# A gated memory and a feed-forward layer on one core: step 3's value products move ahead of the gate transposes, and some loads, conversions and reads are put at other places

## The chip, the cores and the metric

The kernel runs on one core of a Trainium2 chip. The metric is the device time of one execution in microseconds. Before the change its median over three runs is 487.62 us. The core has five engines that each take their instructions in program order: TensorE (PE; its weight loads are listed apart as PEld), VectorE (DVE), ScalarE (ACT), GpSimd (POOL) and SyncE (SP), which here only issues DMA transfers. They wait for each other through semaphores. SBUF is the on-chip memory, PSUM the banks into which TensorE writes, DRAM the memory outside.

## What is computed

For each of 4 batches and 8 heads a recurrence runs over 768 tokens with head size 40; its output goes through a feed-forward layer of width 320 to 2048 to 320.

```
for t in range(S):                          # S = 768, for each b, h
    m_new  = maximum(f[t] + m, i[t])
    f_stab = exp(f[t] + m - m_new);  i_stab = exp(i[t] - m_new);  m = m_new
    C = f_stab * C + i_stab * outer(v[t], k[t])     # 40 x 40
    n = f_stab * n + i_stab * k[t]
    y[t] = sigmoid(o[t]) * (C @ q[t]) / maximum(abs(n @ q[t]), 1)
x = y as (4 * 768, 320)                     # tokens by (head, channel)
h = x @ w_in                                # 3072 x 2048
g = maximum(h, 0) + log1p(exp(-abs(h)))     # softplus
out = g @ w_out                             # 3072 x 320
```

All of it is in fp32.

## The kernel before, in words

**The recurrence** is worked in chunks of 128 tokens. A step is one chunk of one batch with all 8 heads; there are 24, s = 0 to 23. A name such as `3_0` or `0_4` is batch and chunk of a step: step 3 is `3_0`, step 4 is `0_1`, steps 6, 7 and 8 are `0_3`, `0_4` and `0_5`, step 10 is `1_2`. Three steps make one tile of 384 tokens; there are 8 tiles. In a step the decay factors between the tokens (`fb`, loaded from DRAM by `decays`, L436) go through a scan on VectorE (L445, two halves of 4 heads) into the decay matrix `pw`; the scores `sp` (L519, TensorE) multiply it (L521); the value products give the output before normalisation; `cp` (L496) is what the chunk adds to the state, and `cn` is the new state (copied at L503 by ScalarE for a first chunk, added at L501 by VectorE otherwise). Steps up to 5 are "plain" (`plain_step`): value products `yp` (L553), normaliser `nq` (L559 to L561), product with the output gate `sig` (L562, GpSimd) and `x` (L565), then transposes into the tile's operand X (L630 to L636). Steps from 6 on are "wide" (`wide_step`): products with the old state `iq` (L572, read at L575), value products `yq` (L583, read at L588), the result written to DRAM (`yd`, L595) and read back in another layout (`yx`, `nw`, L599 to L603), then normalised (L607 to L610) and put into X (L618 to L622). Queries and keys of a wide step are loaded as a leading part (`hiq`, `hik`, L391) and a remainder (`loq`, `lok`, L405) which are made from one load per tile (L295, `prepare`).

**The feed-forward layer** works on (tile, block) pairs (t, f), with 16 blocks of 128 hidden columns for each tile: 8 matmuls `hp` (L1000), softplus twice on ScalarE (L872 `gh`, L873), a remainder `gl` on VectorE (L876), and 9 matmuls `po` (L966) in three groups of three: `woh` with `gh`, `wol` with `gh`, `woh` with `gl`. An fp32 operand is held as a leading part and a remainder there too, and products of the two remainders are left out. Block 0 to 9 of tile 0 come first, then all 16 of tile 1, then the last 6 of tile 0; the half sums of tile 0 lie in DRAM in between (`halves`, written at L1027, read back by `get_halves` at L1035, added at L1041). Tiles 2 to 7 follow. The weights are converted piece by piece while this runs: `convert(u, 0)` makes `wih` and `wil` for blocks 2u and 2u+1, `convert(u, 1)` makes `woh` and `wol`. Each goes through ScalarE (L212 `mag`, L215 `sg`), VectorE (L217, L219, both on `sg`), ScalarE (L250, L254 or L265) and GpSimd (L257, L259 or L267).

**What sets the order.** `products()` counts the feed-forward matmuls, n. Everything else is a generator that says at which n it wants to go on; `tick(n)` lets those go on whose number has come. Each engine then executes its instructions in the order in which they were written. So tables of numbers set the order of the program on each engine, and when something happens is left to the waits: `GR` for the gates, `CW` and `CO` for the conversions, `W_...`, `SOON` and `SCAN` for wide steps, `SPD`, `IQD`, `YQD` for how many matmuls a read follows its products.

**The gates of later chunks** are transposed on TensorE once (`pg`, L189 and L191) and copied to `gT` by ScalarE (L193, L194); L196 loads the factors `flast` by which a state decays over a chunk.

**A pair of PSUM banks** serves `cp`, `pg`, `yp`, `sp`, `iq`, `yq` by turns: each new tile takes the other bank of the two, but a name in `again` takes the same bank as the tile ahead of it. A tile can be written once what read its bank's last tile is done.

Of the kernel before, what the change touches and what calls it, by code (L numbers as in the profile page):

```python
# [39 lines left out]
def mlstm_moe_kernel(  # L40
# [28 lines left out]
    class Pair:  # L69


        last = 1
        again = "sp1_0_1", "yp0_1"

        def tile(self, shape, dtype, tag, name, **_):
            self.last ^= name not in self.again
# [72 lines left out]
        nc.scalar.copy(gT[:, 0, 0, :], pg)  # L149
        yield  # L150

    GR = [4, 9, 8, 30, 47, 41, 43, 26]

    def later_gates():

# [4 lines left out]
        nc.sync.dma_start(ig, gates[1, :, L:])  # L160
        yield GR[0]
        m = p2.tile([NCHAIN, w + 1], F32, tag="eg", name="m")
        nc.vector.tensor_copy(m[:, 0:1], m_end)
        nc.vector.tensor_tensor_scan(m[:, 1:], fg, ig, m[:, 0:1], ALU.add, ALU.max)
        yield GR[0]
        nc.gpsimd.tensor_tensor(fg, fg, m[:, 0:w], op=ALU.add)
        nc.gpsimd.tensor_tensor(fg, fg, m[:, 1:], op=ALU.subtract)
        nc.gpsimd.tensor_tensor(ig, ig, m[:, 1:], op=ALU.subtract)
        yield GR[1]
        nc.scalar.activation(fg, fg, AF.Exp)  # L170
        nc.scalar.activation(ig, ig, AF.Exp)
        yield GR[2]
        d1 = p1.tile([NCHAIN, w], F32, tag="loq", name="d1")
# [5 lines left out]
        fc = d1  # L179
        yield GR[7]  # L180
        nc.vector.tensor_tensor_scan(fc, fg, d1, 0.0, ALU.mult, ALU.add)
        nc.vector.tensor_copy(fl_s, fc[:, L - 1 : w : L])
        yield GR[3]
        nc.sync.dma_start(fl_d, fl_s)
# [130 lines left out]
    NH = 2 * NG  # L315
# [54 lines left out]
    def load(z):  # L370
        t, n, gs = z.t, z.n, slice(z.g * D, (z.g + 1) * D)
        if t < PLAIN:

            if z.s < NG:
                room, tags = (p1, ("loq", "lok")) if z.s == 2 else (p2, ("qst", "kst"))
                z.qst = room.tile([128, H, L], F32, tag=tags[0], name=f"qst{n}")
                z.kst = room.tile([128, H, L], F32, tag=tags[1], name=f"kst{n}")
                padded[z.s] = z.qst, z.kst
                with tc.issue_after(eye.ins):
                    (nc.gpsimd if z.s == 2 else nc.vector).memset(z.qst, 0.0)  # L380
                    nc.gpsimd.memset(z.kst, 0.0)
            else:
                z.qst, z.kst = padded[z.s % 2]
            nc.sync.dma_start(z.qst[0:D], qk[t, 0, gs])
            nc.sync.dma_start(z.kst[0:D], qk[t, 1, gs])
        else:
            (qh, ql), (kh, kl) = parts[t]
            z.qst = p2.tile([D3, H, L], F32R, tag="qst", name=f"qst{n}")
            z.kst = p2.tile([D3, H, L], F32R, tag="kst", name=f"kst{n}")
            for r, to, part in ((0, z.qst, qh), (0, z.kst, kh), (1, z.qst, qh), (2, z.kst, kh)):  # L390
                nc.sync.dma_start(to[r * D : (r + 1) * D].bitcast(F32), part[gs].bitcast(F32))  # L391
        if t > 0:
            z.old = None
            if z.c > 0 and not stays(z.b, z.c - 1):
                z.old = p2.tile([D3, H, E2], F32, tag="cn", name=f"pk{n}")
                for r in range(3 if t >= PLAIN else 1):
                    nc.sync.dma_start(z.old[r * D : (r + 1) * D], park[z.b])
        if z.s != NG:
            load_values(z)

    def load_low(z):

        gs = slice(z.g * D, (z.g + 1) * D)
        for r, to, part in ((1, z.kst, parts[z.t][1][1]), (2, z.qst, parts[z.t][0][1])):
            nc.sync.dma_start(to[r * D : (r + 1) * D].bitcast(F32), part[gs].bitcast(F32))  # L405
# [16 lines left out]
    def decays(z):  # L422

        z.fbs = []
        h0 = z.b * H
        for i in range(2):
            if z.s < NG:
                fb = ps_h.tile([128, HG, L], F32, tag="hp", name=f"fb{z.n}_{i}")
                for j in range(HG):
                    h = h0 + i * HG + j  # L430
                    nc.tensor.matmul(
                        fb[:, j, :], ident[:, h : h + 1].broadcast_to([128, 128]), fg0, start=True, stop=True
                    )
            else:
                fb = p2.tile([128, HG, L], F32, tag="fb", name=f"fb{z.n}_{i}")
                nc.sync.dma_start(fb, fz_d[z.c, h0 + i * HG : h0 + (i + 1) * HG, :].partition_broadcast(128))  # L436
            z.fbs.append(fb)
# [36 lines left out]
    def stays(b, c):  # L474

        return ORDER.index((b, c + 1)) <= ORDER.index((b, c)) + 2
# [43 lines left out]
        yield 1 if k == 2 * NG + 1 else 2 if i and z.t == 1 else SPD  # L520
        nc.vector.tensor_tensor(z.pws[i], sp, z.pws[i], op=ALU.mult)  # L521

    SPD, IQD, YQD = 5, -8, 3

    def out_gate(z):
        if z.s < NH:
# [291 lines left out]
    def rel(g):  # L818
        for r in g:
            if type(r) is int:  # L820
                yield -1000 - r

    def wide_step(z):
        if z.s != NH + 2:
            yield W_FB
            decays(z)
        yield SOON.get(z.s, W_LOAD)
        load(z)
        yield SOON.get(z.s, W_LOW - 8) + 8
        load_low(z)  # L830
        if z.s == NH + 2:
            decays(z)
        last = z.c == NC - 1
        yw = values_wide(z)

        def y():
            for r in yw:
                if r == "write":
                    return
                yield r  # L840

        c = new_state(z)
        ev = [(SCAN.get(z.s, W_SCAN), lambda: decay(z)), (W_Y, lambda: load_decays(z))]
        if not last:
            ev += [(W_CN, lambda: old_state(z)), (W_VW, lambda: last_decays(z)), (W_VW, lambda: state_values(z))]
        if z.c > 0:
            ev += [(W_CS, lambda: stack(z))]
        ev += [(W_SP0, lambda: scores(z, 0)), (W_SP1, lambda: scores(z, 1))]
        if not last:
            ev += [(W_CP, lambda: state(z)), (W_CP + 6, lambda: next(c)), (W_CD + 6, lambda: next(c))]  # L850
        if z.c > 0:
            ev += [(W_IQ0, lambda: inter_wide(z, 0)), (W_IQ1, lambda: inter_wide(z, 1))]
        ev += [(W_VI if z.s > NH else W_CP, lambda: gate_values(z)), (W_YQ, y), (W_YD, lambda: next(yw, None)), (W_RD, lambda: read_wide(z))]

        d = AWAY
        ev += [(W_FIN + d - 1, lambda: finish_wide(z)), (W_FIN + d, lambda: end_wide(z))]
        ev.sort(key=lambda e: e[0])
        for w, f in ev:
            yield w
            r = f()  # L860
            if hasattr(r, "__next__"):
                yield from rel(r)

    SOON = {NH + 1: -62, NH + 2: -66}
    SCAN = {NH + 1: -30, NH + 2: -30}
    AWAY = 18

# [11 lines left out]
    CW = [-4, -15, 8, 12, 13, 26]  # L879
    CO = [0, 5, 8, 13, 17, 22]  # L880

    def convert(u, i):
        g = (weights_out if i else weights)(u)
        for w in (CO[:4] + [16, 21] if (u, i) == (0, 1) else CO if i else CW[:5] + [22] if u == 1 else CW):
            yield w
            next(g, None)

    def fetch(i):
        yield 20
        fetch_next()  # L890
# [21 lines left out]
    def start(g, base):  # L912
        nonlocal order
        order += 1
        resume(g, base, 0, order)
# [98 lines left out]
    SPLIT = 10  # L1014
# [16 lines left out]
    def get_halves():  # L1031
        yield 0
        for j in range(NG):
            sums[j] = result_tile(0, j)
            nc.sync.dma_start(sums[j], halves[j])  # L1035
# [24 lines left out]
    with in_order():  # L1060
        for k, (u, i) in enumerate(tensors[AHEAD:]):
            if k < 2:
                at = (-8, -4)[k]
            else:
                at = (17 - 2 * 34, 26 - 34 + 10 * (u == 4))[i] + 34 * u if u < SPLIT // 2 else (168, 192)[i] + 48 * (u - SPLIT // 2)
            start(convert(u, i), at)
            start(fetch(i), at)
        start(first_states(), 0)
        LEAD, TS = 174, 16 * 17
        EARLIER = 26  # L1070
        before = -1000
        for s in range(NG, NS):
            z = steps[s] = Step(s)
            if z.wide:
                base = TS * z.t - LEAD - EARLIER - TS * (NG - 1 - z.g) // NG if z.t > WIDE else (183, 264, 344)[z.g]
                if z.g == 0:
                    start(prepare(z.t), (base - 145, before - 54, before - 90)[min(z.t - WIDE, 2)])
                before = base
            else:
                base = [0, 40, 76][s - NG]  # L1080
            start(whole(z), base)
        for t in range(WIDE, NT):
            start(wide_gates(t), TS * (t - 1) + GP + 70 * (t == WIDE))
        start(warm_block(4, 5), 0)
        start(warm_block(9, 4), 0)
        start(get_halves(), TS + 17 * SPLIT + 40)
        zs = first_tile()
        products()

# [36 lines left out]
```

## Time and profile before

| | |
|---|---|
| runs | 487.62, 484.41 and 489.94 us, median 487.62 |
| profiled execution | 489.94 us, of which the profile's span covers 488.2 |
| mean granted TensorE clock | 0.985 |
| TensorE busy | 468.6 us, 96% of the span |
| VectorE, ScalarE, GpSimd busy | 66%, 44% and 45% |
| TensorE instructions | 3444 |

The profiled execution is the slowest of the three runs; 1.7 us of it lie outside the span. A busy TensorE includes time at a lower clock. In the profile's rows "L" and a number is a line of the kernel above, names are given as output `<-` inputs without the numbers of step and buffer, and a bracket at a row's end is the idle time of the engine just before and what ended it. SPq rows are DMA issues on SyncE.

### The profile page before, as it was taken

How to read it: one execution, taken by the hardware profiler on the slowest of the kernel's cores; microseconds unless marked ns; L12 is line 12 of the kernel's file. 1: busy time of each engine (PE TensorE's matmuls, PEld its weight loads, DVE VectorE, ACT ScalarE, POOL GpSimd, SP SyncE). 2: the span in 40 equal slices, each digit the busy share in tenths (PEclk: the TensorE clock that was granted, in tenths of full speed). 3: DMA queues.
4: the chain of work that ended last, by engine and by line, in shares of the span. 5: the costliest groups of instructions: out<-in, count | busy, mean ns of one | idle time of the engine just before them, and what ended most of it. 6: DMA issues, size and time to landing. Idle time of an engine off the chain costs nothing.

```text
span 488.2 us, 9355 instructions
## 1 busy us (share of the span) xinstructions
PE 468.6 (96%) x3444; PEld 447.6 (92%) x3444; DVE 324.6 (66%) x517; ACT 216.6 (44%) x424; POOL 218.0 (45%) x303
## 2 busy tenths in 40 slices
PE   8997999898989989999999999999999999999996
PEld 7976998798888989999999999999999999999996
DVE  8878787868678748568568659568757757542211
ACT  1656446555934524264343635263424433334232
POOL 8375558368875232652383344634375234110000
PEclk9999699999999989999999999999999999999999
DMA  6948955689957695678655874668657571001001
GB/s 180 290 146 257 232 187 183 180 236 271 209 159 200 183 238 148 174 198 214 204 159 176 218 223 122 182 193 223 170 161 198 138 225 45 17 24 42 0 1 41
DMA packets 45608, 81.11 MB, mean 166 GB/s; under 512 B 6626, under 2 KB 23482, under 8 KB 45562
## 3 DMA queue, kind: packets, MB, share of 16 engines
q1 hardware_dynamic: 38218, 68.80, 50.7%
q0 software_dynamic: 4320, 8.26, 6.7%
q10 hardware_dynamic: 3024, 3.44, 2.1%
q8 instruction: 27, 0.44, 0.4%
q14 instruction: 19, 0.16, 0.1%
HBM read 52.38 MB, written 8.80 MB: 125 GB/s over the span
## 4 chain that ended last, share of the span: by engine, by line
PE 71%; DMA 8%; DVE 5%; ACT 2%; issue 2%; SPq 1%; POOL 1%; ACTq 0%; DVEq 0%
PE hp L1000 31%; PE po L966 30%; PE yq L583 3%; PE sp L519 3%; PE cp L496 2%; PE iq L572 2%; DMA nw<-yd 2%; DMA wr<-in_w_in 1%; DMA wo<-in_w_out 1%; DMA y<-fc_d 1%; DMA fb<-fz_d 1%; DMA qst<-loq 1%; DVE sgo L217 1%; SPq L391 1%; DVE pw L445 0%
## 5 line engine op out<-in xcount | busy, mean ns | idle before, releaser
L1000 PE MATMUL hp<-X,wih 128*128 128x384 f32 x768 | 182.0, 341 | 0.4 <-ACT X L634 0.4
L872 ACT ACTIVATE gh<-hp 128x384 fp32r<-128x384 f32 x128 | 62.7, 490 | 168.5 <-PE hp L1000 149.9
L1000 PEld LDWEIGHTS hp<-X,wih 128*128 128x128 f32 x768 | 133.0, 189 | 2.2 <-issue 0.9
L876 DVE TENSOR_TENSOR gl<-hp,gh 128x384 fp32r<-128x384 f32 x128 | 70.2, 549 | 56.4 <-ACT hp L873 56.0
L966 PE MATMUL po<-woh,gh 128*128 128x320 f32 x384 | 83.5, 315 | 1.6 <-ACT gh L872 1.1
L966 PE MATMUL po<-woh,gl 128*128 128x320 f32 x384 | 84.3, 314 | 0.1
L966 PE MATMUL po<-wol,gh 128*128 128x320 f32 x384 | 83.0, 315 | 0.9 <-POOL wol L267 0.9
L445 DVE TENSOR_TENSOR_SCAN pw<-fb,ident 128x512 f32<-128x512 f32 x48 | 71.5, 1529 | 0.1
L1000 PE MATMUL hp<-X,wil 128*128 128x384 f32 x256 | 69.5, 344 | 0.0
L966 PEld LDWEIGHTS po<-woh,gh 128*128 128x128 f32 x384 | 65.3, 189 | 3.2 <-ACT gh L872 1.4
L966 PEld LDWEIGHTS po<-wol,gh 128*128 128x128 f32 x384 | 62.3, 190 | 2.5 <-issue 1.2
L966 PEld LDWEIGHTS po<-woh,gl 128*128 128x128 f32 x384 | 63.4, 190 | 0.6 <-DVE gl L876 0.4
L873 ACT ACTIVATE hp<-hp 128x384 f32<-128x384 f32 x128 | 62.2, 486 | 0.0
L595 POOL DMA_DIRECT2D yd<-y x36 | 20.8, 580 | 85.8 <-DVE y L588 84.0
L1000 PEld LDWEIGHTS hp<-X,wil 128*128 128x128 f32 x256 | 46.1, 189 | 1.1 <-issue 1.0
L575 DVE TENSOR_TENSOR y<-iq,y 41x512 f32<-41x512 f32 x36 | 24.5, 682 | 30.4 <-PE iq L572 27.9
L519 PEld LDWEIGHTS sp<-qst,kst 120*128 120x128 f32 (+1 forms) x240 | 33.6, 198 | 5.9 <-issue 3.6
L519 PE MATMUL sp<-qst,kst 120*128 120x128 f32 (+1 forms) x240 | 34.1, 277 | 4.8 <-DMA qst<-loq 2.3
L521 DVE TENSOR_TENSOR pw<-sp,pw 128x512 f32<-128x512 f32 x48 | 32.0, 682 | 5.2 <-PE sp L519 4.9
L620 ACT CAST X<-eg 128x384 fp32r<-128x384 f32 x18 | 9.2, 514 | 52.1 <-DVE eg L618 52.1
L472 POOL TENSOR_TENSOR vw<-vt,gw 128x328 f32<-128x328 f32 x19 | 15.6, 822 | 36.0 <-DVE gw L466 25.0
L501 DVE TENSOR_TENSOR cn<-cn,cp 40x328 f32<-40x328 f32 x16 | 7.8, 486 | 29.9 <-POOL cn L487 29.3
(131 smaller groups left out, 596.9 us busy)
## 6 DMA issues: line engine op xcount, KB each, us to landing
fb<-fz_d SPq DMA_DIRECT2D x42, 256.0 KB
vt<-in_vko SPq DMA_DIRECT2D x23, 324.0 KB
qst<-hiq SPq DMA_DIRECT2D x36, 160.0 KB
kst<-hik SPq DMA_DIRECT2D x36, 160.0 KB
wo<-in_w_out SPq DMA_DIRECT2D x8, 640.0 KB
wr<-in_w_in SPq DMA_DIRECT2D x8, 512.0 KB
eg<-in_oT SPq DMA_DIRECT2D x6, 576.0 KB
yd<-y POOLq DMA_DIRECT2D x36, 96.0 KB, 3.3
```

What stands on the lines that cost most here:

```text
L445: nc.vector.tensor_tensor_scan(pw.rearrange(flat), fb.rearrange(flat), ident4.rearrange(flat), 0.0, ALU.mult, ALU.add)
L472: nc.gpsimd.tensor_tensor(z.vw, v1, z.gw.broadcast_to([128, H, E]), op=ALU.mult)
L519: nc.tensor.matmul(sp[:, j, :], z.kst[:, h, :], z.qst[:, h, :], start=True, stop=True)
L521: nc.vector.tensor_tensor(z.pws[i], sp, z.pws[i], op=ALU.mult)
L575: nc.vector.tensor_tensor(y, iq, y, op=ALU.mult)
L583: nc.tensor.matmul(yq[e0:e1, p, :], z.via[:, h * E : h * E + e1 - e0], z.pws[h // HG][:, h % HG, :], start=True, stop=True)
L595: nc.gpsimd.dma_start(rows[i], z.y[i * PP : i * PP + EP])
L872: nc.scalar.activation(gh, hp, AF.Softplus)
L873: nc.scalar.activation(hp, hp, AF.Softplus)
L876: nc.vector.tensor_tensor(gl, hp, gh, op=ALU.subtract)
L966: nc.tensor.matmul(po[j], a[:, j * 128 : (j + 1) * 128], w[:, f, :], start=(first and left[j] == 2), stop=(last and left[j] == 0),)
L1000: nc.tensor.matmul(hp, a, r, start=(i == 0), stop=(i == len(seq) - 1))
```

## The change

Seven numbers or tables are changed and one generator is written differently; no instruction is added or taken away.

```
-        again = "sp1_0_1", "yp0_1"
+        again = "sp0_0_1", "sp1_0_1", "yp0_1"
-    GR = [4, 9, 8, 30, 47, 41, 43, 26]
+    GR = [4, 9, 8, 30, 50, 47, 48, 27]
-    SPD, IQD, YQD = 5, -8, 3
+    SPD, IQD, YQD = 5, -8, 1
     def wide_step(z):
-        if z.s != NH + 2:
-            yield W_FB
-            decays(z)
-        yield SOON.get(z.s, W_LOAD)
-        load(z)
-        yield SOON.get(z.s, W_LOW - 8) + 8
-        load_low(z)
-        if z.s == NH + 2:
-            decays(z)
+        soon, low = SOON.get(z.s, (W_LOAD, W_LOW))
+        at = [(W_FB + 12 * (z.s == NH + 2), decays), (soon, load), (low, load_low)]
+        for w, f in sorted(at, key=lambda e: e[0]):
+            yield w
+            f(z)
-    SOON = {NH + 1: -62, NH + 2: -66}
+    SOON = {NH + 1: (-96, -54), NH + 2: (-66, -58)}
     def convert(u, i):
         g = (weights_out if i else weights)(u)
-        for w in (CO[:4] + [16, 21] if (u, i) == (0, 1) else CO if i else CW[:5] + [22] if u == 1 else CW):
+        for w in (CO[:4] + [16, 21] if (u, i) == (0, 1) else CO[:4] + [23, 27] if (u, i) == (1, 1) else CO if i
+                  else CW[:5] + [22] if u == 1 else CW[:3] + [9, 10, 26] if u == 2 else CW):
...
-                at = (17 - 2 * 34, 26 - 34 + 10 * (u == 4))[i] + 34 * u if u < SPLIT // 2 else (168, 192)[i] + 48 * (u - SPLIT // 2)
+                at = (17 - 2 * 34, 26 - 34 + 6 * (u == 4))[i] + 34 * u if u < SPLIT // 2 else (168, 198)[i] + 48 * (u - SPLIT // 2)
...
-        start(get_halves(), TS + 17 * SPLIT + 40)
+        start(get_halves(), TS + 17 * SPLIT + 95)
```

Here NH is 6, so that `NH + 1` and `NH + 2` are steps 7 and 8. In words: the gate transposes and their copies come later (`GR`), and with them `sp0_0_1` joins the names that stay on the bank of the tile ahead; the remainder load and the output conversion of piece 1 come later and piece 2's VectorE half earlier (`convert`); the output conversions of piece 4 come 4 matmuls earlier, those of pieces 5 to 7 come 6 later; a wide value product is read 1 matmul after it instead of 3; step 7's leading loads come 34 matmuls earlier; step 8's decays go behind the next tile's loads; the half sums are loaded 55 matmuls later.

Below are three places in the program's order. The first is on GpSimd, where the feed-forward layer reaches block 2 of tile 0: `wol_99<-sgo1` is the remainder of `w_out` for blocks 2 and 3, `sig3_0` the output gate of step 3, and `vw0_1` the weighted values of step 4. Before:

```order
L259 TENSOR_TENSOR wih_96<-sgi2_477,wih_96 64x128 x2
L267 TENSOR_TENSOR wol_99<-sgo1_576,woh_98 128x640
L562 TENSOR_TENSOR sig3_0_467<-sig3_0_467,nq3_0_660 128x320
L472 TENSOR_TENSOR vw0_1_671<-vt0_1_527,gw0_1_668 128x328
L484 MEMSET cn0_1_724 128x336
```

And on GpSimd at that place after the change:

```order
L259 TENSOR_TENSOR wih_96<-sgi2_477,wih_96 64x128 x2
L562 TENSOR_TENSOR sig3_0_467<-sig3_0_467,nq3_0_658 128x320
L472 TENSOR_TENSOR vw0_1_670<-vt0_1_527,gw0_1_667 128x328
L267 TENSOR_TENSOR wol_99<-sgo1_576,woh_98 128x640
L484 MEMSET cn0_1_724 128x336
```

The remainder `wol` has moved behind step 3's `sig` and step 4's `vw`. At the same place TensorE has the following before (`pg` are the gate transposes, `yp3_0` step 3's value products, `po` the output products of block 1):

```order
L189 MATMUL pg_606<-ident4_79,ig_117 128x32 x5
L191 MATMUL pg_606<-ident4_79,d1_426 128x32 x2
L966 MATMUL po0_0_0_551<-woh_98,gh0_1_504 128x320
L966 MATMUL po0_0_1_552<-woh_98,gh0_1_504 128x320
L966 MATMUL po0_0_2_553<-woh_98,gh0_1_504 128x320
L966 MATMUL po0_0_0_551<-wol_99,gh0_1_504 128x320
L966 MATMUL po0_0_1_552<-wol_99,gh0_1_504 128x320
L553 MATMUL yp3_0_633<-vi3_0_571,pw3_0_0_439 128x41 x4
L553 MATMUL yp3_0_633<-vi3_0_571,pw3_0_1_441 128x41 x4
L966 MATMUL po0_0_2_553<-wol_99,gh0_1_504 128x320
```

TensorE at that place after the change (the lines behind the diff are numbered 4 lower there, so that L962 is L966 above):

```order
L962 MATMUL po0_0_0_551<-woh_98,gh0_1_504 128x320
L962 MATMUL po0_0_1_552<-woh_98,gh0_1_504 128x320
L962 MATMUL po0_0_2_553<-woh_98,gh0_1_504 128x320
L962 MATMUL po0_0_0_551<-wol_99,gh0_1_504 128x320
L962 MATMUL po0_0_1_552<-wol_99,gh0_1_504 128x320
L553 MATMUL yp3_0_622<-vi3_0_571,pw3_0_0_439 128x41 x4
L553 MATMUL yp3_0_622<-vi3_0_571,pw3_0_1_441 128x41 x4
L962 MATMUL po0_0_2_553<-wol_99,gh0_1_504 128x320
L189 MATMUL pg_636<-ident4_79,ig_117 128x32 x5
L191 MATMUL pg_636<-ident4_79,d1_426 128x32 x2
```

The value products and the transposes have changed places, and with them their banks: the tile ahead of both is `cp3_0`, whose bank `yp3_0` had to share before and `pg` has to share now. The third place is on SyncE, ahead of step 10's scores: `halves` are tile 0's half sums, `cn1_1` the state that step 10 starts from, `lok3` and `loq3` the remainders of tile 3. Before:

```order
L420 DMA vt1_2_1925<-in_vko 128x648
L1035 DMA ob0_0_1931<-halves_102 128x320
L1035 DMA ob0_1_1933<-halves_102 128x320
L1035 DMA ob0_2_1935<-halves_102 128x320
L507 DMA cn1_1_1856<-cn1_1_1856 40x336
L508 DMA cn1_1_1856<-cn1_1_1856 40x336
L405 DMA kst1_2_1920<-lok3_1450 40x1024
L405 DMA qst1_2_1919<-loq3_1448 40x1024
L295 DMA loq4_2041<-in_qk 120x1024
L295 DMA lok4_2043<-in_qk 120x1024
L350 DMA y1_2_2097<-fc_d_89 64x4x128
```

And on SyncE at that place after the change:

```order
L420 DMA vt1_2_1925<-in_vko 128x648
L507 DMA cn1_1_1856<-cn1_1_1856 40x336
L508 DMA cn1_1_1856<-cn1_1_1856 40x336
L405 DMA kst1_2_1920<-lok3_1444 40x1024
L405 DMA qst1_2_1919<-loq3_1442 40x1024
L295 DMA loq4_2035<-in_qk 120x1024
L295 DMA lok4_2037<-in_qk 120x1024
L1031 DMA ob0_0_2068<-halves_102 128x320
L1031 DMA ob0_1_2070<-halves_102 128x320
L1031 DMA ob0_2_2072<-halves_102 128x320
L350 DMA y1_2_2097<-fc_d_89 64x4x128
```

The three loads of half sums have moved behind six others. Besides these, on VectorE the read of step 6's `yq` (L588) and one `gl` stand ahead of `w_out` piece 6's conversion (L217, L219) instead of behind it, the state sum `cn0_4` (L501) stands ahead of piece 7's, and L219 of piece 4 stands ahead of a part of X (L636). On ScalarE, step 3's place has `mag` and `sg` of `w_in` piece 3 (L212, L215) ahead of the two copies to `gT`, and these ahead of `woh` (L265), where `woh` came first and `mag`, `sg` last. On SyncE, step 7's leading loads and values (L391, L420) stand ahead of `w_in` piece 7 and step 7's decays, behind `w_out` piece 5, and step 8's decays (L436) stand behind the two loads of tile 3 (L295) instead of ahead of them.

More of the change, by code (lines that the diff above doesn't have):

```diff
@@ L883, in convert @@
         g = (weights_out if i else weights)(u)
-        for w in (CO[:4] + [16, 21] if (u, i) == (0, 1) else CO if i else CW[:5] + [22] if u == 1 else CW):
+        for w in (CO[:4] + [16, 21] if (u, i) == (0, 1) else CO[:4] + [23, 27] if (u, i) == (1, 1) else CO if i else CW[:5] + [22] if u == 1 else CW[:3] + [9, 10, 26] if u == 2 else CW):
             yield w
```

## The prediction

> **What bounds the kernel now.** I read the page first for the busy shares, then TensorE's waits, then busy time by stages, and last the timeline and the chain around the waits that the change touches.
>
> ```profile
> PE 468.6 (96%) x3444; PEld 447.6 (92%) x3444; DVE 324.6 (66%) x517; ACT 216.6 (44%) x424; POOL 218.0 (45%) x303
> PEclk9999699999999989999999999999999999999999
> ```
>
> TensorE is busy 468.6 of 488.2 us, so only two things can be won: its idle time, and the time at a lower clock, which the strip shows in two places (6 and 8 tenths). Its waits, longest first:
>
> ```profile
> PE yp L553 <- issue: 2.6, 1, 2.6
> PE sp L519 <- DMA qst<-loq: 2.3, 1, 2.3
> ...
> PE sp L519 <- DVE y L588: 1.3, 1, 1.3
> PE po L966 <- ACT gh L872: 1.1, 1, 1.1
> PE iq L572 <- DVE cn L501: 1.1, 1, 1.1
> ...
> PE po L966 <- POOL wol L267: 0.9, 1, 0.9
> ...
> PE po L966 <- ACT woh L265: 0.5, 1, 0.5
> ```
>
> Columns: total, times, longest. Now the stages (length, busy time of each engine, then the granted clock, the DMA engines' share and GB/s):
>
> ```profile
> 49.00:58.00 9.00, 9.00 (x38) 9.00 (x39) 7.31 (x12) 2.38 (x5) 4.51 (x6) 0.52 1.01 234
> 100.00:130.00 30.00, 27.05 (x217) 24.93 (x216) 24.04 (x32) 18.05 (x34) 22.97 (x26) 1.00 0.93 247
> 172.00:178.00 6.00, 5.17 (x25) 5.20 (x26) 1.94 (x3) 1.35 (x3) 3.25 (x5) 0.72 1.04 240
> 178.00:300.00 122.00, 122.00 (x931) 117.14 (x930) 85.44 (x138) 51.62 (x101) 54.27 (x86) 1.00 0.67 186
> ```
>
> The two longest waits are each followed by slow time: 9.00 us at 0.52 lose 9.00 x 0.48 = 4.3 us of full-clock work, 6.00 us at 0.72 lose 1.7. From 178 to 300 TensorE has no gap. So whatever TensorE has gained by 178 us should reach the end; what is gained earlier can be lost at a later wait whose cause does not move with it.
>
> **Part 1, the exchange at 46 to 58 us (`GR`, `again`, conversion of piece 1).**
>
> ```profile
> 45.90 0.45 PE L966 MATMUL po<-wol,gh 128*128 128x320 f32 x2
> 48.99 3.61 PE L553 MATMUL yp<-vi,pw 128*128 128x41 f32 x16 [2.63 <-issue]
> ...
> 58.19 0.61 PE L966 MATMUL po<-wol,gh 128*128 128x320 f32 x3
> ...
> 48.48 0.42 ACT L503 COPY cn<-cp 40x328 f32<-40x328 f32 x1
> ...
> 49.62 3.90 DVE L445 TENSOR_TENSOR_SCAN pw<-fb,ident 128x512 f32<-128x512 f32 x2
> ...
> 50.60 1.83 POOL L267 TENSOR_TENSOR wol<-sgo,woh 128x640 fp32r<-128x640 f32 x1 [0.59 <-ACT woh L265]
> 54.55 0.72 POOL L562 TENSOR_TENSOR sig<-sig,nq 128x320 f32<-128x320 f32 x1 [2.12 <-DVE gw L466]
> 55.23 0.74 POOL L472 TENSOR_TENSOR vw<-vt,gw 128x328 f32<-128x328 f32 x1
> ```
>
> The wait called "issue" ends at 48.99, just when the copy that frees `cp3`'s bank ends (48.48 + 0.42 = 48.90); `yp` shares that bank. On the other bank `yp` needs no wait, and TensorE reaches `pg`, which now waits for the copy. This 2.63 us goes. What is late next is on GpSimd: `wol`, needed by the `po` group that ran at 58.19, used to run at 50.60. Now it stands behind `sig` and `vw`, which wait for VectorE's scans. The scans began at 49.62 and took 3.90 beside `wol`; with `wol` gone from beside them they should take about what the pair below takes.
>
> ```profile
> 127.80 2.32 DVE L445 TENSOR_TENSOR_SCAN pw<-fb,ident 128x512 f32<-128x512 f32 x2
> ```
>
> Taking 49.3 as their start (a little earlier than before, since VectorE has nearly the same work ahead): 2.3 for the scans, 1.0 from their end (49.62 + 3.90 = 53.52) to `sig` at 54.55 as before, 0.72 + 0.74 for `sig` and `vw`, then `wol`, some 1.5 where it took 1.83 beside a scan. That is about 55.6. TensorE, without its wait of 2.63 and the 4.3 us that the slow clock took, would want it at 58.19 - 6.9 = 51.3. So **a new wait of some 4 us** takes the old one's place, and the `po` group starts at 55.6 in place of 58.19: 2.6 earlier. Since waits of 2.6 and 2.3 us were both followed by slow clock, I charge this one too, at the smaller of the two prices: 2.6 - 1.7 = **0.9 us gained**. Bounds: no slow clock, +2.6; the larger price of 4.3, 2.6 - 4.3 = -1.7.
>
> **Part 2, VectorE's L219 of piece 4 ahead of X.**
>
> ```profile
> 87.81 0.55 DVE L636 TENSOR_TENSOR X<-xp,X 128x384 fp32r<-128x384 f32 x1
> ...
> 89.90 0.71 PE L966 MATMUL po<-woh,gh 128*128 128x320 f32 x3 [0.53 <-ACT woh L265]
> ```
>
> L219 no longer has the 0.55 us of L636 ahead of it, and TensorE's wait of 0.53 for `woh` depends on it. I take **0.4**, between 0 and 0.55. Moving the other pieces' ScalarE and GpSimd halves by a few matmuls I cost at 0: those two engines are idle over half the span, and their queues' order moves under TensorE's `hp` work; without that cover, a piece costs one `wol`, at most 1.8.
>
> **Part 3, step 6's `yq` read, step 7's loads, `cn0_4` (109 to 140 us).** The waits of 1.3 (`sp` for L588), 1.1 (`iq` for `cn` L501) and 0.4 (`cp` for `vw` behind them) go, since each reader now stands ahead of a conversion that itself waited. That is 2.8 on TensorE. But a lead has to pass this:
>
> ```profile
> 134.07 1.01 DVE L607 SCALAR_TENSOR_TENSOR nm<-nw 128x128 f32<-128x128 f32 x1 [0.88 <-DMA nw<-yd]
> ...
> 139.40 0.71 PE L966 MATMUL po<-woh,gh 128*128 128x320 f32 x3 [1.11 <-ACT gh L872]
> ...
> 126.42 7.63 DMA nw<-yd
> ...
> 119.19 1.79 SPq L436 DMA_DIRECT2D fb<-fz_d  x2
> ...
> 121.09 0.38 SPq L295 DMA_DIRECT2D loq<-in_qk  x1
> 122.13 1.02 SPq L295 DMA_DIRECT2D lok<-in_qk  x1
> ```
>
> At 139.40 TensorE waits for an activation whose engine had been busy putting step 6 into X; that chain (`nw` from DRAM 7.63 us, then five operations on VectorE) runs from 126.42, in a stretch with the DMA engines 0.93 busy. Step 7's loads start earlier, which thins that stretch, but step 8's decays `fb` now queue behind two loads of 480 KB (120 x 1024 x 4 bytes): 0.96 MB at the 247 GB/s of that stretch is 3.9 us. The scans that need them began at 127.80, and `nm` stands behind the scans on VectorE. The two about cancel, so I take **0 net**: the 2.8 us are won at 115 to 127 and given back by 140. Upper bound 2.8. For the lower one: `fb` was issued at 119.19 and now comes behind `lok`, whose issue ended at 123.15, 4.0 later; the scans would begin at 131.8 and end at 134.1, and between them and `nm` VectorE has four more operations:
>
> ```profile
> 130.04 0.52 DVE L876 TENSOR_TENSOR gl<-hp,gh 128x384 fp32r<-128x384 f32 x1
> 130.60 0.69 DVE L575 TENSOR_TENSOR y<-iq,y 41x512 f32<-41x512 f32 x1
> 131.39 0.69 DVE L588 TENSOR_TENSOR y<-yq,y 112x512 f32<-112x512 f32 x1
> 132.63 0.56 DVE L876 TENSOR_TENSOR gl<-hp,gh 128x384 fp32r<-128x384 f32 x1 [0.56 <-ACT hp L873]
> ```
>
> With their 2.5 us `nm` starts at 136.6, 2.5 later than 134.07, and TensorE's wait at 139.40 becomes 2.5 longer net of all lead; with a slow stretch at the larger price, 4.3, this is -6.8.
>
> **Part 4, the half sums behind step 10's loads (160 to 178 us).**
>
> ```profile
> 159.17 0.49 DVE L501 TENSOR_TENSOR cn<-cn,cp 40x328 f32<-40x328 f32 x1 [2.35 <-POOL cn L487]
> ...
> 160.02 5.28 SPq L1035 DMA_DIRECT2D ob<-halves  x3
> ...
> 167.71 0.71 SPq L405 DMA_DIRECT2D qst<-loq  x1
> ...
> 167.71 4.98 DMA qst<-loq
> ...
> 172.83 0.63 PE L519 MATMUL sp<-qst,kst 120*128 120x128 f32 x4 [2.31 <-DMA qst<-loq]
> ...
> 179.08 0.93 DVE L1041 TENSOR_TENSOR ob<-po,ob 128x320 f32<-128x320 f32 x2 [2.06 <-PE po L966]
> ```
>
> SyncE held the loads of half sums for 5.28 us until their buffers were free, with step 10's four loads queued behind them: the last, `qst<-loq`, went out at 167.71 and landed 4.98 later, and `sp` waited 2.31 for it. Now the four can go once `cn` is there (159.17 + 0.49 = 159.66): four issues of 0.7 put `qst<-loq` at about 161.8, and with the same 4.98, even with 2 us more, it lands by 169, ahead of 170.5 where TensorE began to wait. The wait of 2.31 goes and with it its slow stretch of 1.7: **+4.0**. The half sums queue behind two more issues, still go out at about 165.5 when their buffers are free, and are needed at 179.08: free. Bounds 0 (another load is late in its place) and 4.0.
>
> [...]
>
> **The sum.** 0.9 + 0.4 + 0 + 4.0 = 5.3 us against the profiled execution's 489.94: 484.6. That execution is the slowest of three, 2.3 above the median, and I don't know how much of this the changed kernel's runs would share; I take half, 1.2, off every case below: **483.4**.
>
> **The rivals.** (a) The new wait of part 1 stays short, or starts no slow stretch (+2.6 in place of 0.9), and part 3 keeps some 1.5 of its 2.8: 5.3 + 1.7 + 1.5 = 8.5, so 480.2. For it: step 7's earlier loads; nothing shows a rule for the clock that would spare a wait of 4 us. (b) The new wait costs as much clock as the old one (-1.7 in place of 0.9): 5.3 - 2.6 = 2.7, so 486.0. For it: the light products there, 16 of 41 columns, are the same as in the stretch at 0.52. (c) The change does not do what it says in part 4: the DMA engines, 1.04 busy from 172 to 178, bring step 10's data no earlier: 5.3 - 4.0 = 1.3, so 487.4. Against it: the issue itself was 5.28 late. (d) Slower: step 8's decays land late behind the 0.96 MB, the delay goes through VectorE to step 6's X, and TensorE's wait at 139.40 is long enough for a slow stretch like that at 49 to 58. That is the -6.8 of part 3: 0.9 + 0.4 - 6.8 + 4.0 = -1.5, so 490.2. For it: the order on SyncE, and DMA engines 0.93 busy there. Against it: step 7's loads, 0.96 MB too with its values (4 x 160 and 324 KB), now leave that stretch ahead of it. It decides from the point where `fb` holds the scans up by more than the 1.4 us that VectorE idled there (0.56 ahead of `gl`, 0.88 ahead of `nm`); no row shows how full the queue then is.
>
> **How the numbers follow.** Forecast 0.38, (a) 0.24, (b) 0.15, (c) 0.11, (d) 0.12. One per cent of 487.62, about what a measurement of this kernel can tell from no change, is 4.9: faster below 482.7, slower above 492.5. The forecast lies 0.7 inside "the same" and spreads by some 2, so a third of it counts as faster; with (a) that is 0.13 + 0.24 and a little from spread of the runs (484.41 to 489.94): 0.41 faster. Slower by over 1% needs (d) with part 1 at its lower bound too (2.6 more, 492.8): 0.06, half of (d). The rest is 0.53. The range leaves out the outer part of (a) and of (d): 478.8 to 489.0.
>
> **What would show it.** In the changed profile `yp` L553 should have no wait; `po` should wait for `wol` L267 by some 4 us at 51 to 56, with a stretch of about half clock behind it; `sp` should not wait for L588 and `iq` not for `cn` before 130; DVE's scan near 125 to 130 should wait for `fb`; `qst<-loq` should go out near 158 to 162, no wait and no slow clock follow at 170, and the last of the loads of half sums land before `ob` L1041. The prediction is wrong if the wait for `wol` is under 2 us, if the lead at 130 is still there at 140, or if a wait for step 10's data remains.

## The result: half a per cent slower, and the profile after

The changed kernel takes 490.01 us in the median of 20 runs (488.67 to 491.48), the kernel before 487.60 in 20 runs beside them (483.97 to 493.49). The ratio is 1.0054, 95% interval 1.0033 to 1.0076: slower by a little over half a per cent. The forecast was 483.4 us in 478.8 to 489.0, so the time lies outside the range. The ratios here and below leave out executions more than 1.5% above the fastest of their kernel, so they are not the quotients of the medians.

The profiled execution of the changed kernel is its shortest run (488.67 us, span 486.9), that of before one of its longer ones. Their spans therefore stand the other way round than the medians, and what follows is read from places in the two traces, not from the two spans.

TensorE's busy time and the clock strip on the page, after the change:

```profile
PE 465.8 (96%) x3444; PEld 445.6 (92%) x3444; DVE 324.0 (67%) x517; ACT 217.0 (45%) x424; POOL 218.6 (45%) x303
PEclk9999899999979999999999999999999999999999
```

The two dips of before, at slices 5 and 15, have become one at slice 5 and one at slice 12, from 134 to 146 us. TensorE's waits, longest first:

```profile
PE sp L519 <- DVE y L575: 5.7, 1, 5.7
PE po L962 <- POOL wol L267: 5.7, 2, 5.0
...
PE xp L630 <- DVE x L565: 1.7, 2, 1.4
```

The waits of before for `issue`, for step 10's remainder, for L588, for `cn` and for `woh` are all gone. The 5.0 us for `wol` is the new wait that part 1 forecast. **The 5.7 us at `sp` behind L575 is not in the forecast.** Stages of the changed kernel around it (same columns as before):

```profile
112.00:128.00 16.00, 15.86 (x127) 15.04 (x126) 10.37 (x17) 10.99 (x21) 14.65 (x20) 1.00 0.96 245
128.00:144.00 16.00, 10.30 (x56) 10.04 (x56) 11.61 (x15) 7.22 (x12) 5.97 (x7) 0.79 0.62 148
160.00:182.00 22.00, 22.00 (x176) 21.10 (x175) 14.57 (x26) 10.80 (x19) 9.62 (x18) 1.00 0.86 244
```

and the same stretches of the kernel before:

```profile
112.00:128.00 16.00, 13.23 (x98) 12.22 (x97) 12.45 (x18) 10.44 (x22) 13.35 (x19) 1.00 0.92 233
128.00:144.00 16.00, 14.77 (x105) 13.77 (x104) 12.61 (x17) 10.73 (x17) 11.64 (x12) 1.00 0.76 187
160.00:182.00 22.00, 19.69 (x139) 18.71 (x138) 13.58 (x24) 7.37 (x14) 7.07 (x12) 0.92 0.83 209
```

From 112 to 128 TensorE is busy 2.6 us longer (15.86 against 13.23), as part 3 meant. From 128 to 144 it is busy 10.30 us in place of 14.77, and that at a clock of 0.79: 5.7 us of idling where it had 1.2. The slow clock there is 3.4 us (16.00 x 0.21), but part of it falls into the idling and costs nothing. What counts is the time behind the wait:

```profile
136.10:144.00 7.90, 7.90 (x41) 7.90 (x42) 7.11 (x11) 2.53 (x6) 3.78 (x5) 0.76 0.65 167
```

TensorE has no gap there, so 7.90 x 0.24 = 1.9 us are lost to the clock. The same `hp` matmuls start 2.0 us earlier than in the kernel before at 130 us and 3.9 later at 141: 5.9 us go in between. From 160 to 182 TensorE has no gap and full clock, as part 4 meant (though the kernel before has that too in its second profile, run 8). So the loss is in one place. What was late there, in the changed kernel's timeline, on SyncE, VectorE and TensorE:

```profile
118.76 0.45 SPq L295 DMA_DIRECT2D loq<-in_qk  x1
119.32 1.31 SPq L295 DMA_DIRECT2D lok<-in_qk  x1
120.68 0.97 SPq L436 DMA_DIRECT2D fb<-fz_d  x2
...
131.52 3.36 DVE L445 TENSOR_TENSOR_SCAN pw<-fb,ident 128x512 f32<-128x512 f32 x2 [6.30 <-DMA fb<-fz_d]
...
135.36 0.69 DVE L575 TENSOR_TENSOR y<-iq,y 41x512 f32<-41x512 f32 x1
...
136.10 1.12 PE L519 MATMUL sp<-qst,kst 120*128 120x128 f32 x4 [5.70 <-DVE y L575]
```

and in its chain of waits (start, length, what):

```profile
120.68 10.82 DMA fb<-fz_d
```

Step 8's decays go out behind 0.96 MB of tile 3's queries and keys and land 10.82 us after their issue, at 131.50. VectorE has the scans next in its order and stands still for 6.30 us, with every later instruction behind it, among them L575, which reads step 7's `iq` out of one of the two shared PSUM banks. TensorE's next `sp` needs that bank. It reached it at 130.40 and started at 136.10.

### The profile page after: what moved, and what is told of

Its sections match the earlier page's. It is cut to its first block, busy times and chain, and to the rows that moved or that the text cites. A ratio compares the mean times of both kernels' runs of the same rounds, so it can differ in the third digit from the quotient of the medians.

```text
span 486.9 us, 9344 instructions
## 1 busy us (share of the span) xinstructions
PE 465.8 (96%) x3444; PEld 445.6 (92%) x3444; DVE 324.0 (67%) x517; ACT 217.0 (45%) x424; POOL 218.6 (45%) x303
## 4 chain that ended last, share of the span: by engine, by line
PE 73%; DMA 13%; DVE 9%; issue 2%; ACT 2%; SPq 1%; POOL 0%; DVEq 0%; ACTq 0%
PE hp L996 32%; PE po L962 31%; DMA fb<-fz_d 3%; DMA wr<-in_w_in 3%; PE yq L583 3%; PE sp L519 3%; PE cp L496 2%; DMA qst<-hiq 2%; PE iq L572 2%; DVE pw L445 1%; DVE sgi L219 1%; DMA kst<-in_qk 1%; DVE sgi L217 1%; DMA cn<-cn 1%; DVE sgo L217 1%
## 5 line engine op out<-in xcount | busy, mean ns | idle before, releaser
L962 PE MATMUL po<-wol,gh 128*128 128x320 f32 x384 | 83.1, 316 | 5.7 <-POOL wol L267 5.7
L962 PE MATMUL po<-woh,gl 128*128 128x320 f32 x384 | 84.3, 314 | 0.0
L962 PE MATMUL po<-woh,gh 128*128 128x320 f32 x384 | 82.9, 313 | 0.2 <-ACT ob0h L1021 0.2
L962 PEld LDWEIGHTS po<-wol,gh 128*128 128x128 f32 x384 | 62.2, 189 | 7.5 <-POOL wol L267 6.2
L962 PEld LDWEIGHTS po<-woh,gh 128*128 128x128 f32 x384 | 65.1, 188 | 1.4 <-ACT ob0h L1021 0.6
L962 PEld LDWEIGHTS po<-woh,gl 128*128 128x128 f32 x384 | 63.3, 190 | 0.3 <-issue 0.2
L575 DVE TENSOR_TENSOR y<-iq,y 41x512 f32<-41x512 f32 x36 | 24.5, 682 | 26.5 <-PE iq L572 24.2
L521 DVE TENSOR_TENSOR pw<-sp,pw 128x512 f32<-128x512 f32 x48 | 32.0, 682 | 5.9 <-PE sp L519 5.2
L501 DVE TENSOR_TENSOR cn<-cn,cp 40x328 f32<-40x328 f32 x16 | 7.8, 486 | 32.1 <-POOL cn L487 31.5
```

Of the source, the lines that this page charges most:

```text
L575: nc.vector.tensor_tensor(y, iq, y, op=ALU.mult)
L962: nc.tensor.matmul(po[j], a[:, j * 128 : (j + 1) * 128], w[:, f, :], start=(first and left[j] == 2), stop=(last and left[j] == 0),)
```

## Experiments

Each edit is to the changed kernel unless another is named; ratios are to the kernel before on the same chip, with 95% intervals. The first four share a chip, so do the next four, the next four and the last four.

**1. Step 8's decays back ahead of the two loads.** Nothing else moves on any engine.

```
-        at = [(W_FB + 12 * (z.s == NH + 2), decays), (soon, load), (low, load_low)]
+        at = [(W_FB + 7 * (z.s == NH + 2), decays), (soon, load), (low, load_low)]
```

> The changed kernel with one edit: step 8's two decay loads (fb, 2 x 256 KB) stand ahead of tile 3's two loads (loq, lok, 2 x 480 KB) on SyncE again. Nothing else moves on any engine. Theory 1 (late decays are the loss): in the changed kernel VectorE's scans waited 6.30 us for fb, TensorE 5.70 us at sp behind it, and the clock was at half for some 7 us after it. Here fb should land 4 us earlier, near 127.5, TensorE should have no wait over 1.5 us between 125 and 140, no slow clock there, and the median should fall by some 6.5 us, from 490.0 to about 483.5. Theory 2 (the stretch is bound by its bytes and the delay only moves to loq and lok or to nw): a wait of like size appears by 145, the median stays within 1.5 us of 490.

Measured: 486.38 us in 12 runs, 0.9993 (0.9956 to 1.0029); VectorE at that place and its waits for `fb`:

```profile
129.08 3.71 DVE L445 TENSOR_TENSOR_SCAN pw<-fb,ident 128x512 f32<-128x512 f32 x2 [0.85 <-DMA fb<-fz_d]
```

The wait of 6.30 is 0.85, that of 5.70 on TensorE is 0.6, and the clock from 128 to 148 is 1.00. The loss is gone, and with it theory 2: the longest wait that follows by 145 is 1.8 us, for `gh`. The median fell less than the 6.5 expected, about 3 by the two ratios (1.0054 and 0.9993, on different chips): its runs fall into a group at 483.7 to 485.7 and one at 487.1 to 490.0. The profiled execution is the longest run and has this stretch around the wait for `wol`:

```profile
44.00:72.00 28.00, 22.96 (x149) 21.64 (x149) 17.34 (x27) 12.15 (x25) 14.27 (x13) 0.76 0.81 232
```

0.76 over 28 us is 6.7 us, of which 6.4 fall behind the wait (0.57 over the 14.97 us from 57.03 on, without a gap) and are lost; the changed kernel's own profile has 0.94 there with the same wait, 1.7 us. The timed repeat on another chip follows as run 14.

**2. The same two loads late in the kernel before.** The edit is the converse of the first:

```
         if z.s == NH + 2:
+            yield -52
             decays(z)
```

> The kernel before with one edit: step 8's two decay loads go behind tile 3's two loads on SyncE, nothing else moves. Theory 1: fb lands about 4 us later, VectorE's scans wait 3 to 4 us, TensorE waits about 3 us at sp near 132 and has one or two windows of half clock (1.7 to 3.4 us lost): 4 to 6 us slower, 492 to 494. Theory 2 (the late decays hurt only together with the earlier lead of the changed kernel): within 1.5 us of 487.6.

Measured: 489.75 us, 1.0059 (1.0022 to 1.0096). This one move alone makes as much of a loss as the whole change. VectorE and TensorE there:

```profile
131.01 1.22 DVE L445 TENSOR_TENSOR_SCAN pw<-fb,ident 128x512 f32<-128x512 f32 x1 [4.10 <-DMA fb<-fz_d]
...
136.25 1.11 PE L519 MATMUL sp<-qst,kst 120*128 120x128 f32 x4 [4.79 <-DVE y L575]
```

The same wait in the same place, 4.79 us. The time rose by 3.2 us, less than the 4 to 6 expected. The old wait of 2.31 us at step 10 is not among its waits, but that need not make the difference: this wait is there in one profile of five only (run 8).

**3 and 5. The `wol` of blocks 2 and 3 early again,** beside edit 1: in run 3 with its `woh`, in run 5 without, so that ScalarE keeps the changed order.

```
-  CO[:4] + [23, 27] if (u, i) == (1, 1) else CO if i else ...
+  CO if i else ...                                               # run 3
+  CO[:4] + [23, 23] if (u, i) == (1, 1) else CO if i else ...    # run 5
```

> As the first run, and besides, ScalarE's woh and GpSimd's wol for blocks 2 and 3 stand where the kernel before has them, ahead of step 3's sig and step 4's vw. Theory 1 (the wait of 5.0 us for wol and its window of half clock are a real loss of part 1): that wait goes below 1 us, and the median falls 2 to 3 us under the first run's, to about 481; not the whole 5 + 1.7, since step 5's decays land late anyway. Theory 2 (the wait for wol is cover for something that is late in any case, such as the scans or step 4's state): another wait of 3 us or more stands between 50 and 70, and the median is within 1 us of the first run's.

> As the first run (step 8's decays back ahead), and of the conversion for blocks 2 and 3 only GpSimd's wol moves back ahead of step 3's sig and step 4's vw; ScalarE keeps the changed order, with woh behind the two copies to gT. Theory 1 (wol's place behind sig, and not the place of woh, made the wait of 5.0 us): no wait over 1 us for wol between 50 and 60, none over 0.5 us for gT either (it was 2.4 in the third run, where woh stood ahead of the copies and itself waited 1.6 us), and a median at or under the third run's, 481 to 483 against 486.5 for the kernel before. Theory 2: woh, now last on ScalarE, comes too late for GpSimd, the wait is 2 us or more, and the median is 484 or above.

Measured: 483.04 us, 0.9939 (0.9905 to 0.9974), and 483.2, 0.9927 (0.9897 to 0.9958). In both, the wait for `wol` is at most 0.7 us. In run 3 `sp` waits 2.4 us for the copies to `gT` instead, in run 5 it waits 2.2 for L521. So both kernels beat the kernel before, and a shorter wait of another kind takes the place of the 5.0, under the 3 us of run 3's theory 2. Run 3 is 3.3 us under run 1, a little more than theory 1 asked, but run 1's median lies between its two groups; runs 14 and 15 repeat the comparison for run 5's kernel.

**4. The half sums late in the kernel before, alone.**

```
-        start(get_halves(), TS + 17 * SPLIT + 40)
+        start(get_halves(), TS + 17 * SPLIT + 95)
```

> The kernel before with one edit: the three loads of half sums go behind step 10's state and remainder loads and tile 4's two loads on SyncE, nothing else moves. Theory 1 (part 4 of the prediction): the wait of 2.31 us at sp near 170 and the window of half clock behind it go, the median falls by 4.0 us to about 483.6. Theory 2: a wait for another load takes its place, or the wait is not there in most executions: within 1 us of 487.6.

Measured: 485.37 us, 0.9980 (0.9949 to 1.0012): the interval reaches from 2.5 us gained to 0.6 lost, so no gain is shown, and 4.0 is outside it. What was meant happens: `qst<-loq` goes out at 162.14 and `sp` does not wait.

**6. ScalarE's order behind run 5:** `mag` and `sg` of `w_in` piece 3 three matmuls later.

```
-  at = (17 - 2 * 34, ...
+  at = (17 - 2 * 34 + 3 * (u == 3), ...
```

> As the fifth run, and ScalarE's mag and sg of w_in piece 3 come 3 matmuls later, behind the two copies to gT and woh. If ScalarE's order is what sets this place, both copies and woh are 1.5 us earlier and TensorE's waits between 48 and 58 fall below 1 us together, with little or no half clock there: 1 to 3 us faster than the fifth run, near 480. If step 5's decays, which land late, set the time behind it, the gain is taken back by 70 and the median is within 1 us of the fifth run's.

Measured: 483.51 us, 0.9926 (0.9896 to 0.9957), level with run 5. The first expectation fails: `sp` still waits 2.2 us for L521, so ScalarE's order is not what sets this place. The clock from 44 to 72 is 1.00 in its profile, but that is not the edit's doing: it is 1.00 in run 15 too, which is run 5's kernel, and 0.82 in run 5. The median is what the second expectation said; that step 5's decays are the reason is not shown.

**7. Run 3 with the half sums early,** the converse of run 4 in a kernel that was expected to come to 170 us earlier.

> The third run with one edit: the loads of half sums are back ahead of step 10's state and remainder loads. Theory 1 (part 4 is worth its wait and its window of half clock whenever TensorE comes early): the wait at sp for step 10's remainder is back, 3 us or more since TensorE leads by 3 us more than in the kernel before, with half clock behind it, and the median is 4 us or more above the third run's. Theory 2 (that wait is often absorbed, as the fourth run's small gain suggests): under 2 us above it.

Measured: 484.57 us, 0.9948 (0.9917 to 0.9979), 1.5 above run 3, with the intervals overlapping. In its profile TensorE waits 2.15 us for step 6's X (`gh`, near 139), so that it comes to step 10 no earlier than in the kernel before, and has no wait there:

```profile
167.47 0.71 SPq L405 DMA_DIRECT2D qst<-loq  x1
...
170.48 0.63 PE L519 MATMUL sp<-qst,kst 120*128 120x128 f32 x4
```

In the kernel before `qst<-loq` went out at 167.71 and TensorE stood from 170.52 to 172.83. With the same order, about the same issue and the same arrival there is no wait here: this transfer took at most 3.0 us, that one 4.98.

**8. The kernel before once more, for a second profile.**

> The kernel before, unchanged, for a second profile. [...]

Measured: 490.17 us. Its waits on TensorE:

```profile
PE yp L553 <- issue: 2.6, 1, 2.6
...
PE sp L519 <- DVE y L588: 2.1, 1, 2.1
PE sp L519 <- DVE y L575: 1.5, 1, 1.5
```

The wait for `yp` is again 2.6, the clock from 44 to 64 is 0.74 in both profiles. But **the wait of 2.31 us for step 10's remainder is not there**: the load and TensorE both come some 3 us later.

```profile
170.88 0.71 SPq L405 DMA_DIRECT2D qst<-loq  x1
...
173.97 0.58 PE L519 MATMUL sp<-qst,kst 120*128 120x128 f32 x4
```

TensorE comes 3.1 us after the issue, where it came 2.8 after it in the first profile (170.52 and 167.71), and finds the data there: the transfer took at most 3.1 us, not 4.98. The wait is not there in runs 2, 7 and 10 either, which have the half sums early too. In these four `sp` starts 3.0 to 4.3 us behind the issue, so one profile of five has the wait, and it is the one with the slowest transfer.

**9 and 10. Part 1 undone beside edit 1, and part 1 alone on the kernel before.** Edit 9 puts `GR`, `again`, `CO` for piece 1 and `CW` for piece 2 back; edit 10 makes these four alone.

> The first run's kernel (step 8's decays back ahead) with part 1 undone as a whole: gate transposes, their copies, the bank rule and the conversions of pieces 1 and 2 as in the kernel before, so that parts 2 to 4 stand alone. Theory 1 (in medians part 1 with its wait of 5.0 us for wol loses about what the old wait of 2.63 lost): within 1 us of the first run, 0.999 of the kernel before. Theory 2 (part 1 is itself a loss that hid a gain of the other parts): 2 us or more faster than the first run, ratio 0.995 or less.

> The kernel before with part 1 alone (gate transposes behind the value products, bank rule, conversions of pieces 1 and 2). By the prediction's term 0.9 us faster, bounds -1.7 to +2.6 gained. By theory 1: within 1 us of the kernel before, the wait for wol 5.0 us again. By theory 2: slower by 1.5 us or more.

Measured: run 9 483.1 us in 6 runs, 0.9889 (0.9837 to 0.9940); run 10 488.64, 0.9999 (0.9965 to 1.0033). Alone, part 1 moves nothing that 12 runs can tell: the wait for `wol` of 5.0 us, which is there, and its slow clock cost about what the wait of 2.63 and its slow clock cost. Run 9 is clearly faster than the kernel before, but its distance to run 1 is one between two chips, which run 14 and run 16 settle.

**11. Step 7's leading loads back to where they were.**

```
-    SOON = {NH + 1: (-96, -54), NH + 2: (-66, -58)}
+    SOON = {NH + 1: (-62, -54), NH + 2: (-66, -58)}
```

> The changed kernel with step 7's leading loads and values back where the kernel before has them, behind w_in piece 7 and step 7's decays. The prediction let these 0.96 MB, gone from the stretch ahead, cancel the 0.96 MB put ahead of step 8's decays. If the earlier loads do thin that stretch, fb lands some 3 to 4 us later here than in the changed kernel, VectorE waits 9 us or more for it and the median rises by 3 us or more, to 493. If they do not (the stretch from 90 to 130 is busy either way, and SyncE issues fb only behind waits of its own), fb lands at the same time within 1 us and the median is within 1.5 us of the changed kernel's.

Measured: 491.48 us, 1.0066 (1.0033 to 1.0099), which does not differ from the changed kernel's 1.0054. The scans start later, but so does all that is ahead of them:

```profile
123.43 10.64 DMA fb<-fz_d
...
134.09 3.28 DVE L445 TENSOR_TENSOR_SCAN pw<-fb,ident 128x512 f32<-128x512 f32 x2 [6.81 <-DMA fb<-fz_d]
```

`fb` lands 2.6 us later than in the changed kernel's first profile (2.0 and 1.7 later than in runs 12 and 13), between the two expectations, but only because it is issued later. From issue to landing it takes 10.64 us, against 10.82, 10.61 and 10.81 in the changed kernel, so the earlier loads do not thin this stretch. Step 7's first leading load and its values say why, in the changed kernel and then in the kernel before:

```profile
90.64 0.79 SPq L391 DMA_DIRECT2D qst<-hiq  x1
93.82 0.74 SPq L420 DMA_DIRECT2D vt<-in_vko  x1
...
98.55 0.81 SPq L391 DMA_DIRECT2D qst<-hiq  x1
101.76 0.63 SPq L420 DMA_DIRECT2D vt<-in_vko  x1
```

Even in the kernel before they were issued by 102.4, 17 us ahead of `fb` at 119.19. VectorE's wait is 6.81 against 6.30, 7.18 and 7.19 in three profiles of the changed kernel. The earlier loads bring TensorE to this place about as much earlier as they bring `fb` (its wait begins at 132.47 here and at 130.41 there), and so they cannot pay for it.

**12. The changed kernel once more, for a second profile.**

> The changed kernel, unchanged, for a second profile: the waits of 5.0 us for wol and 5.7 us at sp behind step 8's decays should be there again within 0.5 us, with slow stretches of possibly other lengths; the time between 488.7 and 491.5.

Measured: 490.98 us, with 6.12 us at `sp` and 5.0 for `wol`: both waits are there again, within the 0.5 allowed.

**13 to 16. Four kernels on one chip:** the changed one, run 1's, run 5's and run 9's.

> The changed kernel once more, timed on the same chip as the next three, so that part 1 can be priced within one chip. By all so far 1.005 of the kernel before.

> The first run's kernel (step 8's decays back ahead) on that chip. If the late decays cost what the first and second run say, 2.5 to 3.5 us under the changed kernel.

> The fifth run's kernel (decays back ahead, and GpSimd's wol ahead of sig and vw) on that chip. If wol's place alone makes part 1 a loss, 2.5 to 3.5 us under the kernel with the decays back, and level with the next within 1 us. If more of part 1 costs, it is 2 us or more slower than the next.

> The ninth run's kernel (decays back ahead, part 1 undone as a whole) on that chip. The ninth run gave 0.989 against the kernel before and the first run 0.999, on two chips; part 1 alone on the kernel before gave 1.000. If part 1 is a loss beside the other parts, this is 3 us or more under the kernel with the decays back; if the two chips made the difference, within 1.5 us of it.

| on one chip, 12 runs each | median us | to the kernel before (486.79, 35 runs) |
|---|---|---|
| changed | 490.14 | 1.0078 (1.0041 to 1.0115) |
| decays back | 484.27 | 0.9948 (0.9911 to 0.9984) |
| decays back, `wol` early | 483.51 | 0.9942 (0.9909 to 0.9974) |
| decays back, part 1 undone | 483.26 | 0.9923 (0.9894 to 0.9951) |

**Moving two loads of 256 KB back is worth 5.9 us here,** more than the 2.5 to 3.5 expected from runs 1 and 2. Of part 1, wholly undone, 1.0 us is left, and of `wol`'s place alone 0.8, less than the intervals can tell: the two chips made the distance between run 9 and run 1, and part 1 is not shown to be a loss. The last three all beat both kernels. VectorE's scans of step 8 in the last:

```profile
124.64 2.83 DVE L445 TENSOR_TENSOR_SCAN pw<-fb,ident 128x512 f32<-128x512 f32 x2 [1.92 <-DMA fb<-fz_d]
```

They begin 6.9 us earlier than in the changed kernel. Even ahead of the two loads `fb` is waited for by 1.92 us there: in this kernel the load had no slack to give.

## Why the prediction was wrong

**The failing step is part 3's net of 0.** It said that step 8's decays, now behind 0.96 MB, and step 7's loads, 0.96 MB out of the way, "about cancel". Three things were wrong in it.

- The cancelling. The two sets of loads were set against each other as bytes, but step 7's loads had been issued 17 us before `fb` already, and run 11 shows that they take nothing off its way: 10.64 us from issue to landing without their move, 10.61 to 10.82 with it, and the same ratio.
- The size. `fb` was issued at 120.68, only 1.5 us later than before and not 4.0 as the lower bound had it, and took 10.82 us to land. Ahead of the two loads it took at most 5.2 in run 14, 6.6 in run 1, 7.2 in run 16 and 9.3 in run 8. The 0.96 MB ahead of it are 3.9 us at the 245 GB/s of the stretch from 112 to 128; that estimate fits most of these, but they spread too far to bear it out. So the scans began at 131.52, 3.7 us later than before, close to the lower bound's 131.8 by another sum. What TensorE had won (the 2.0 us of lead at 130) became wait on top of that: VectorE was ready at 125.2 and stood for 6.30.
- The place. The prediction let the delay go through `nm` and X to the wait at 139.40, with 1.4 us of VectorE's idling as a cushion. It hit earlier, at `sp`, because the scans stand ahead of L575 on VectorE and L575 frees a PSUM bank. There was no cushion on that way. Case (d) named the transfer and the clock, and put the chance at 0.12 and the price at 6.8; the price was 5.9 in the median on the one chip that timed both, about 3 by runs 1 and 2, with 1.9 of slow clock in place of 4.3 (3.3 in run 12's profile).

The measured 490.01 is close to case (d)'s own 490.2, which the range, ending at 489.0, left out. That closeness is luck in part, since (d) counts part 4's 4.0 as won. The three signs by which the prediction would have called itself wrong did not show: the wait for `wol` is 5.0, the lead at 130 is gone at 141, and no wait for step 10's data is left. None of them asked whether more than the lead is lost.

Without this one move the time is 484.27 in run 14 (486.38 in run 1), against the forecast of 483.4. That is agreement of a sum, not of its terms:

- **Part 1: mechanism right, gain not there.** `yp` does not wait, and `wol` comes late behind `sig` and `vw` as forecast, in the changed kernel's profile:

```profile
53.51 0.72 POOL L562 TENSOR_TENSOR sig<-sig,nq 128x320 f32<-128x320 f32 x1 [3.29 <-DVE gw L466]
54.19 1.33 POOL L472 TENSOR_TENSOR vw<-vt,gw 128x328 f32<-128x328 f32 x1
55.49 2.13 POOL L267 TENSOR_TENSOR wol<-sgo,woh 128x640 fp32r<-128x640 f32 x1
...
57.67 0.94 PE L962 MATMUL po<-wol,gh 128*128 128x320 f32 x3 [4.99 <-POOL wol L267]
```

  The `po` group starts at 57.67, not 55.6, so 0.5 us earlier than before and not 2.6: `vw` and `wol` took 1.33 and 2.13, 1.2 us over what was taken, and the scans started at 49.83, not 49.3. Term 0.9 forecast; alone 0.0 with an interval of 1.6 either way.
- **Part 2: too small to see.** The wait of 0.5 for `woh` is gone; one of 0.4 us for X (L636) is new, so that little of the 0.4 is left.
- **Part 3's other half was undersized.** The waits went, and where `fb` is early most of the lead is not given back by 140: in run 16 TensorE starts the same `hp` matmuls 1.7 us earlier than in the kernel before at 110 us, 4.5 at 130 and 4.1 at 141. In runs 1, 3, 5, 9 and 14 it wins 2.1 to 2.9 over the same stretch and gives back 0.2 to 1.5. In run 16 the chain to X moved too, since `nw` landed earlier (L607 at 130.05 against 134.07).
- **Part 4: the wait was no fixed price.** No wait and no slow clock at 170. But in the changed kernel `qst<-loq` goes out at 167.77, not between 158 and 162: step 10's state and remainder loads begin only at 163.62 in this late kernel. And 4.0 us was the price in one execution; alone the median moved by 1.2 (run 4, not shown to differ from 0) and 1.5 (run 7). Runs 7 and 8 say why: in the same order the transfer mostly takes less than that execution's 4.98 us (at most 3.0 and 3.1), and then there is nothing to wait for.
- **The allowance** of 1.2 for a long profiled execution hardly matters: 484.6 without it and 483.4 with it are both inside the interval around 484.27.

The prediction charged slow clock to part 1's new wait and to part 4's old one because in one execution waits of 2.6 and 2.3 us were both followed by it. In the second profile of the kernel before, the wait of 2.6 us is again followed by slow clock (0.74 from 44 to 64), and so are a wait of 1.69 us in run 2 (0.89 from 112 to 128) and those of 5.0 and 5.7 us in the changed kernel (0.88 from 58 to 72, 0.76 from 136.10 to 144). But a wait does not always bring it: behind 2.2 us at `sp` the clock from 44 to 72 is 0.82 in run 5 and 1.00 in run 15, the same kernel.

## What to carry to other kernels

When a load is moved behind others in an in-order issue queue, work out when it lands (issue behind them, then their bytes at the stage's rate, an estimate that came to 3.9 us here for 0.96 MB at 245 GB/s) and hold that against its reader in that stage. Ask of an earlier load elsewhere whether it would still have been under way then, and whether it brings the reader forward too: here step 7's loads, issued 17 us ahead of `fb` already, left its time to land as it was (10.64 us without their move, 10.61 to 10.82 with it), and TensorE came to its wait 2.1 us earlier with them. Follow the reader's engine through to what it frees: here VectorE's wait of 6.30 us for `fb` kept a PSUM bank from TensorE, which waited 5.70 us for a read that stands two instructions behind the scans. And price a wait from two executions where they are at hand, since it may not be there in the second: the 2.31 us for step 10's remainder were in one profile of five.

## What the runs showed of the chip that was not expected

The price of the same wait in slow clock differs from one execution to the next. With the wait for `wol` at 5.0 us each time, the granted clock from 44 to 72 us was 0.94 in one profile of the changed kernel and 0.88 in two others, and with the decays back 0.76 in run 1 and 0.88 in run 14. From 58 to 72, behind the wait, where TensorE has no gap in any of them, that is 1.4 to 5.9 us lost. The lengths come in steps: in the first profile of the kernel before the clock is 0.50 from 50 to 57, and taken at half clock the 0.94, 0.88, 0.82 and 0.76 over 28 us are 3.4, 6.7, 10.1 and 13.4 us, one to four times the same. The kernel before spread over 9.5 us in 20 runs, the changed one over 2.8. What sets the number of steps stays open.
